# Key transposes in an attention decode kernel: one bf16 tile at a time in place of two packed as fp32

## The chip, the cores and the metric

The kernel runs on one core of one Trainium2 chip. Times are device microseconds of that core. A run that is over 1.5% above the fastest of its kernel counts as slow; ratios compare fast runs with fast runs, while medians are over all runs. TensorE's granted clock is given as a share of full speed; the traces show it at either 1.0 or 0.5, so a mean of 0.8 means that 40% of the time was spent at half speed (181.8 of 447.8 us in the profiled run of before; its clock record starts at 23.6 us, and what lies before counts as full speed).

## The reference, cut to what matters

Two attention layers, A and B, decode one token each for four sequences. Each has 32 query heads over 8 key heads. A attends to all 8192 cached keys, B to the last 2048. All tensors are bf16.

```python
q = (x @ wq).reshape(B, 1, 32, 128).transpose(0, 2, 1, 3)
scores = einsum("bhqd,bhkd->bhqk", q, k) * 128 ** -0.5
p = softmax(scores, axis=-1)
o = einsum("bhqk,bhkd->bhqd", p, v)
out = o.transpose(0, 2, 1, 3).reshape(B, 1, 4096) @ wo
```

The work on the key and value caches is split into 40 *units* of 2 MB of keys and 2 MB of values. Eight are B's; 32 are A's, one for each sequence and key head.

## The kernel before

The cached keys arrive with the key position on the partitions, but the score matmul needs the head dimension there, so TensorE transposes all keys. A unit has 64 key tiles of 128x128. The kernel takes them in eight groups of eight. It views two neighbouring bf16 tiles as one fp32 tile of 128x128 and transposes that, four times a group:

```python
def pe_T(u, k):                                   # unit u, group k
    ...
    for pi in range(4):
        t0 = k * 8 + 2 * pi
        ins = pe.transpose(out=bkf[:, pi * 128:(pi + 1) * 128],          # fp32 PSUM bank
                           in_=K_sbf[:, slot, t0:t0 + 2, :].rearrange("p t d -> p (t d)"),
                           identity=identf[:, :])
    ...
    # PSUM to SBUF: VectorE as int32 for even k, ScalarE as bf16 for odd k
```

A packed transpose puts pairs of head dimensions on one partition, so the query has to be rearranged to match. A small permutation matmul and split copies make `RQA` and `RQB`, and the scores of two tiles are the sum of two matmuls:

```python
for pi in range(4):
    for e in range(2):
        ins = pe.matmul(out=stb[:, t * CPT:(t + 2) * CPT], lhsT=ktv[:, pi, :, e],
                        rhs=rhs, start=(e == 0), stop=(e == 1))
```

The loads use four buffers each for K and V, in one queue.

## Time and profile before

| | before |
|---|---|
| time, median of the first three runs | 449.6 us (448.24 to 449.67) |
| span of the profiled run | 447.8 us |
| mean granted clock | 0.797 |
| TensorE instructions in one turn of the loop | 1316 |
| distance between packed transposes, clock 1.0 / 0.5 | 109 / 213 ns |

The last is the median distance between the starts of neighbouring matmuls of one group. Starts are the safer measure here, because the durations overlap: the mean duration of a packed transpose is 329 ns on the page below.

These are lines of the profile page: busy time of each engine; clock, DMA share and DMA rate in 40 slices of the span; the DMA queue that fetches instructions (packets, MB, share); and the four groups around the transpose (busy us, mean ns of one, then the idle time before them).

```profile
PE 373.4 (83%) x6783; PEld 339.4 (76%) x6783; DVE 195.9 (44%) x451; ACT 179.2 (40%) x202; POOL 40.1 (9%) x126
...
PEclk9996569989886899866596689867875986788596
DMA  8999999999999999999999999999999999999991
GB/s 337 411 415 438 413 421 415 420 421 423 423 422 421 425 422 425 424 429 427 427 427 430 430 424 426 430 428 427 429 426 427 426 430 429 426 424 430 430 403 65
...
q8 instruction: 22, 0.36, 0.3%
...
L341 ACT ACTIVATE KT_sb<-ps 128x1024 bf16<-128x1024 bf16 x160 | 163.0, 1023 | 244.9 <-PE ps L332 243.1
L332 PE MATMUL ps<-identf,K_sb 128*128 128x128 f32 x1280 | 217.1, 329 | 32.9 <-DMA K_sb<-in_A_k_cache_dram 17.5
L332 PEld LDWEIGHTS ps<-identf,K_sb 128*128 128x128 f32 x1280 | 179.0, 170 | 46.2 <-DMA K_sb<-in_A_k_cache_dram 18.6
L340 DVE COPY KT_sb<-ps 128x512 int32<-128x512 int32 x160 | 110.4, 690 | 138.9 <-PE ps L332 137.7
```

The next lines are of the table of windows: busy time of each engine in a stretch, then clock, DMA share and rate.

```profile
core 0: us, PE busy (x) PEld busy (x) DVE busy (x) ACT busy (x) POOL busy (x), PEclk, DMA share, GB/s
...
210.00:290.00 80.00, 72.22 (x1296) 67.13 (x1295) 35.61 (x82) 35.06 (x40) 7.50 (x24) 0.78 1.01 428
290.00:370.00 80.00, 73.63 (x1298) 67.85 (x1298) 35.52 (x82) 35.10 (x40) 7.17 (x24) 0.77 1.01 427
370.00:440.00 70.00, 63.30 (x1085) 57.25 (x1085) 32.03 (x73) 30.63 (x35) 6.74 (x21) 0.76 0.98 413
440.00:448.00 8.00, 5.17 (x126) 4.10 (x126) 2.08 (x7) 0.42 (x1) 0.46 (x2) 0.50 0.01 3
```

Read the DMA columns first. The DMA engines are nearly full from the first slice to the last but one, from the second on at 403 to 438 GB/s, and the kernel ends about 7 us after they go quiet. TensorE looks nearly full too, 72 of 80 us, but at a clock of 0.78 and with waits for keys among its idle time (17.5 us before the transposes). Such an engine may be a second limit or may have slack that was slowed down.

### The profile page before, as it was taken

The page shows a single profiled execution, that of the slowest core. Times are in us where ns is not written, and L with a number is a line of the kernel's source. Part 1 is how long each engine was busy: PE and PEld are TensorE (multiplying, and loading weights), DVE is VectorE, ACT ScalarE, POOL GpSimd, SP SyncE. Part 2 cuts the span into 40 slices and gives each one's busy share as a digit, 9 for nine tenths or more (in the row PEclk, how much of TensorE's full clock was granted, in tenths as well). Part 3 has the DMA queues.
Part 4 walks back from the last instruction along what each step waited for, and adds up shares of the span by engine and source line. Part 5 has one row for each costly group of instructions (what it writes and reads, how often), then busy time and mean ns, then how long its engine had stood idle before and what let it go on. Part 6 is the DMA issues. An engine that isn't in the chain of part 4 may idle for free.

```text
span 447.8 us, 14767 instructions
## 1 busy us (share of the span) xinstructions
PE 373.4 (83%) x6783; PEld 339.4 (76%) x6783; DVE 195.9 (44%) x451; ACT 179.2 (40%) x202; POOL 40.1 (9%) x126
## 2 busy tenths in 40 slices
PE   0685199899676999988998998899889998988997
PEld 0685199768561898878898887879878987878896
DVE  0354055656440455434363444344443544344363
ACT  1163045435330464434264434334442543435261
POOL 1100000001100011000010001000110100010010
PEclk9996569989886899866596689867875986788596
DMA  8999999999999999999999999999999999999991
GB/s 337 411 415 438 413 421 415 420 421 423 423 422 421 425 422 425 424 429 427 427 427 430 430 424 426 430 428 427 429 426 427 426 430 429 426 424 430 430 403 65
DMA packets 17270, 185.01 MB, mean 413 GB/s; under 512 B 1860, under 2 KB 2392, under 8 KB 4824
## 3 DMA queue, kind: packets, MB, share of 16 engines
q1 hardware_dynamic: 15096, 178.27, 94.4%
q10 hardware_dynamic: 2080, 6.30, 3.5%
q8 instruction: 22, 0.36, 0.3%
q14 instruction: 8, 0.07, 0.0%
q0 software_dynamic: 64, 0.01, 0.0%
HBM read 184.56 MB, written 0.01 MB: 412 GB/s over the span
## 4 chain that ended last, share of the span: by engine, by line
DMA 54%; PE 35%; issue 4%; ACT 3%; DVE 2%; POOL 0%; ACTq 0%; POOLq 0%
DMA K_sb<-in_A_k_cache_dram 41%; PE ps L332 19%; DMA W<-in_A_wq_dram 7%; DMA W<-in_B_wo_dram 6%; PE ps L397 6%; PE ps L371 5%; PE ps L483 3%; ACT KT_sb L341 3%; PE ps L278 1%; DVE KT_sb L340 1%; DVE Dt L543 0%; DVE M L505 0%; ACT PT L554 0%; PE ps L474 0%; PE ps L438 0%
## 5 line engine op out<-in xcount | busy, mean ns | idle before, releaser
L341 ACT ACTIVATE KT_sb<-ps 128x1024 bf16<-128x1024 bf16 x160 | 163.0, 1023 | 244.9 <-PE ps L332 243.1
L332 PE MATMUL ps<-identf,K_sb 128*128 128x128 f32 x1280 | 217.1, 329 | 32.9 <-DMA K_sb<-in_A_k_cache_dram 17.5
L332 PEld LDWEIGHTS ps<-identf,K_sb 128*128 128x128 f32 x1280 | 179.0, 170 | 46.2 <-DMA K_sb<-in_A_k_cache_dram 18.6
L340 DVE COPY KT_sb<-ps 128x512 int32<-128x512 int32 x160 | 110.4, 690 | 138.9 <-PE ps L332 137.7
L397 PE MATMUL ps<-PT,V_sb 128*128 128x4 bf16 (+1 forms) x2560 | 76.2, 165 | 3.6 <-DMA V_sb<-in_A_v_cache_dram 1.8
L371 PEld LDWEIGHTS ps<-RQc,KT_sb 128*128 128x128 bf16 x2048 | 72.9, 100 | 4.5 <-ACT KT_sb L341 1.2
L371 PE MATMUL ps<-RQc,KT_sb 128*128 128x8 bf16 x2048 | 74.3, 167 | 0.9 <-ACT KT_sb L341 0.8
L397 PEld LDWEIGHTS ps<-PT,V_sb 128*128 128x128 bf16 x2560 | 70.8, 97 | 3.9 <-DMA V_sb<-in_A_v_cache_dram 2.0
L575 POOL PARTITION_ALL_REDUCE LB<-L x40 | 17.3, 432 | 155.2 <-DVE L L566 155.2
L514 POOL PARTITION_ALL_REDUCE MB<-M x32 | 11.9, 371 | 173.3 <-DVE M L505 173.3
L483 PE MATMUL ps<-W,OL 128*4 128x512 bf16 x60 | 22.5, 537 | 4.8 <-DMA W<-in_B_wo_dram 4.8
L592 DVE TENSOR_TENSOR OTg<-ps,RL 128x4 bf16<-128x4 f32 (+1 forms) x40 | 6.9, 173 | 40.2 <-PE ps L397 40.2
L505 DVE TENSOR_REDUCE M<-ps 128x4 f32<-128x256 f32 (+1 forms) x40 | 19.1, 477 | 10.8 <-PE ps L371 10.8
L566 DVE TENSOR_REDUCE L<-PT 128x4 f32<-128x256 bf16 (+1 forms) x40 | 21.9, 547 | 3.3 <-ACT PT L554 2.8
L371 PE MATMUL ps<-RQB,KT_sb 128*128 128x16 bf16 x512 | 18.6, 171 | 2.1 <-issue 1.2
L371 PEld LDWEIGHTS ps<-RQB,KT_sb 128*128 128x128 bf16 x512 | 17.9, 99 | 3.0 <-issue 1.5
L554 ACT ACTIVATE PT<-Dt 128x256 bf16<-128x256 f32 (+1 forms) x40 | 18.1, 452 | 4.0 <-DVE Dt L543 2.0
L483 PEld LDWEIGHTS ps<-W,OL 128*4 128x4 bf16 x60 | 5.6, 104 | 15.3 <-issue 8.7
L278 PE MATMUL ps<-xT,W 128*128 128x4 bf16 x256 | 7.4, 165 | 10.9 <-DMA W<-in_A_wq_dram 10.6
L278 PEld LDWEIGHTS ps<-xT,W 128*128 128x128 bf16 x256 | 7.0, 101 | 11.1 <-DMA W<-in_A_wq_dram 10.7
L543 DVE TENSOR_TENSOR Dt<-ps,MB 128x256 f32<-128x256 f32 x32 | 13.3, 415 | 0.5 <-POOL MB L514 0.5
L257 PE MATMUL ps<-ident,xo_sb 4*128 4x4 bf16 x8 | 0.6, 170 | 14.2 <-POOL identf L617 14.2
(49 smaller groups left out, 64.6 us busy)
## 6 DMA issues: line engine op xcount, KB each, us to landing
K_sb<-in_A_k_cache_dram SPq DMA_DIRECT2D x32, 2048.0 KB, 32.0
V_sb<-in_A_v_cache_dram SPq DMA_DIRECT2D x31, 2048.0 KB, 36.0
K_sb<-in_B_k_cache_dram SPq DMA_DIRECT2D x16, 1024.0 KB, 28.2
V_sb<-in_B_v_cache_dram SPq DMA_DIRECT2D x16, 1024.0 KB, 28.2
W<-in_B_wq_dram SPq DMA_DIRECT2D x1, 4096.0 KB, 12.9
W<-in_A_wq_dram SPq DMA_DIRECT2D x1, 4096.0 KB, 30.0
W<-in_A_wo_dram ACTq DMA_DIRECT2D x8, 512.0 KB, 10.5
W<-in_B_wo_dram SPq DMA_DIRECT2D x1, 2048.0 KB, 29.1
```

The lines of the kernel that those rows point to most:

```text
L278: ins = pe.matmul(out=bk[:, hl * Bn:(hl + 1) * Bn], lhsT=W1wq[:, c, hq * DH:(hq + 1) * DH], rhs=xT[:, P, c, :], start=(c == 0), stop=(c == ...
L332: ins = pe.transpose(out=bkf[:, pi * 128:(pi + 1) * 128], in_=K_sbf[:, slot, t0:t0 + 2, :].rearrange("p t d -> p (t d)"), identity=identf[ ...
L340: return e.tensor_copy(out=KT_sb.bitcast(I32)[:, tj % NKT, :], in_=bkf.bitcast(I32)[:, :])
L341: return e.activation(out=KT_sb[:, tj % NKT, :], in_=bk[:, :], func=ACTF.Copy)
L371: ins = pe.matmul(out=stb[:, t * CPT:(t + 2) * CPT], lhsT=ktv[:, pi, :, e], rhs=rhs, start=(e == 0), stop=(e == 1))
L397: ins = pe.matmul(out=otb[:, s * CPT:(s + 1) * CPT], lhsT=V_sb[:, vs, t, :], rhs=pt_cols(u, t * CPT, CPT), start=(j == 0), stop=(j == J - 1))
L483: ins = pe.matmul(out=opb[0:Bn, 0:D], lhsT=OL[:, i // REP, i % REP, :], rhs=wo_view[:, wg + i // REP, i % REP, :], start=(P == 1 and first ...
L505: return dve.tensor_reduce(out=M1[:, 0:NC].rearrange("p (s h) -> p s h", h=CPT), in_=stb[:, 0:NT * CPT].rearrange("p (s j h) -> p s h j", ...
L543: return dve.tensor_tensor(out=Dt[:, 0:NT * CPT].rearrange("p (s j h) -> p s j h", s=S, h=CPT), in0=stb[:, 0:NT * CPT].rearrange("p (s j h ...
L554: return act.activation(out=PT[:, u % NPT, 0:NW], in_=Dt[:, 0:NW], func=ACTF.Exp, scale=scale)
L566: return dve.tensor_reduce(out=L1[:, 0:NC].rearrange("p (s h) -> p s h", h=CPT), in_=PT[:, u % NPT, 0:NT * CPT].rearrange("p (s j h) -> p ...
L575: return pool.partition_all_reduce(LB[:, 0:NC], L1[:, 0:NC], channels=128, reduce_op=ReduceOp.add)
```

## The change

The intent is to drop the packing: transpose the eight bf16 tiles one by one, use the query as it is, and remove the permutation matmul, its split copies and their set-up. Two things follow from it. The score matmuls keep their number but are half as wide (4 columns in place of 8 for A). And two matmuls of 512 columns that only add zeros to the projection's bank, and read `RQA` to do so, become eight of 128 columns. The core of the diff is here, with cuts marked:

```diff
-                for pi in range(4):
-                    t0 = k * 8 + 2 * pi
-                    ins = pe.transpose(out=bkf[:, pi * 128:(pi + 1) * 128],
-                                       in_=K_sbf[:, slot, t0:t0 + 2, :].rearrange("p t d -> p (t d)"),
-                                       identity=identf[:, :])
+                for i in range(8):
+                    ins = pe.transpose(out=bk[:, i * 128:(i + 1) * 128], in_=K_sb[:, slot, k * 8 + i, :], identity=ident[:, :])
 ...
-                for pi in range(4):
-                    t = k * 8 + 2 * pi
-                    for e in range(2):
-                        ...
-                        ins = pe.matmul(out=stb[:, t * CPT:(t + 2) * CPT], lhsT=ktv[:, pi, :, e],
-                                        rhs=rhs, start=(e == 0), stop=(e == 1))
+                for i in range(8):
+                    t = k * 8 + i
+                    ...
+                    ins = pe.matmul(out=stb[:, t * CPT:(t + 1) * CPT], lhsT=KT_sb[:, tj % NKT, i * 128:(i + 1) * 128],
+                                    rhs=rhs, start=True, stop=True)
 ...
-        def pe_job_perm(P):      # the permutation matmul and the copies into RQA and RQB; all of it goes
 ...
-            pool.memset(RQA[:, :, :, :, :], 0.0)
-            pool.memset(RQB[:, :, :, :, :, :], 0.0)
-            pool.memset(Dt[:, 0:128], 1.0)
```

More of the change, by code (lines that the diff above doesn't have):

```diff
@@ L112, in bass_concat_heads__gqa_block_cached__sliding_block_cached__decode_kernel @@
         onesb = sb("onesb", [128, 128], BF16)
-        identf = sb("identf", [128, 128], F32)
         NGQ = HQ // REP
         NGG = HKV // SB
-        RQA = sb("RQA", [128, Bn, NGQ, 2, 2 * REP], BF16)
-        RQB = sb("RQB", [128, Bn, NGG, 2, 2, 4 * REP], BF16)
-        RQc = sb("RQc", [128, Bn, 2, 2 * REP], BF16)
+        RQc = sb("RQc", [128, Bn, REP], BF16)
         zt = sb("zt", [128, Bn], BF16)
-        permE = sb("permE", [128, 2, 2, 64], BF16)
         MK = sb("MK", [128, 16], F32)
@@ L159, in bass_concat_heads__gqa_block_cached__sliding_block_cached__decode_kernel @@
         s_Eq, s_rq, s_opc = sm("s_Eq"), sm("s_rq"), sm("s_opc")
-        s_mk0, s_perm = sm("s_mk0"), sm("s_perm")
+        s_mk0 = sm("s_mk0")
         KTB = [0, 1, 2]
@@ L171, in bank_bf @@
             return banks_f[i].bitcast(BF16)
-        K_sbf = K_sb.bitcast(F32)
         W1wq = W1[:, :].rearrange("p (c n) -> p c n", c=DC)
@@ L203, in sem_of @@
             if t == "E":
-                if jobs[key[1]]["kind"] in ("xT", "QP", "perm"):
+                if jobs[key[1]]["kind"] in ("xT", "QP"):
                     return s_Eq
@@ L210, in sem_of @@
                 "ocp": s_ocp, "exp": s_exp, "ar1": s_ar1, "ar2": s_ar2, "setup": s_setup, "pset": s_setup,
-                "mk": s_mk, "acp": s_acp, "mk0": s_mk0, "perm": s_perm, "rq": s_rq, "OPJc": s_opc,
+                "mk": s_mk, "acp": s_acp, "mk0": s_mk0, "rq": s_rq, "OPJc": s_opc,
             }[t]
@@ L231, in bass_concat_heads__gqa_block_cached__sliding_block_cached__decode_kernel @@
         xt_idx = {}
-        perm_idx = {}
         ol_idx = {}
@@ L286, in pe_job_QP @@
             return dict(eng="dve", fn=efn, waits=[("T", idx)], inc=("E", idx))
-        def pe_job_perm(P):
-            idx = new_job("perm", "dve", P=P)
-            perm_idx[P] = idx
-            bk = bank_f(KTB[jobs[idx]["bank"]])
-            def fn(pe):
-                ins = None
-                for e in range(2):
-                    ins = pe.matmul(out=bk[:, e * Bn * HQ:(e + 1) * Bn * HQ],
-                                    lhsT=permE[:, e, :, :].rearrange("p t i -> p (t i)"),
-                                    rhs=QT[:, P, :, :].rearrange("p b h -> p (b h)"), start=True, stop=True)
-                return ins
-            op("pe", fn, waits=[("E", qp_idx[(P, NQP - 1)]), ("perm",), bankfree(idx)], inc=("T", idx))
-            def efn(dve):
-                ins = None
-                for e in range(2):
-                    for tl in range(2):
-                        src = bk[64 * tl:64 * tl + 64, e * Bn * HQ:(e + 1) * Bn * HQ]
-                        if P == 0:
-                            ins = dve.tensor_copy(
-                                out=RQA[64 * tl:64 * tl + 64, :, :, e, REP * tl:REP * tl + REP],
-                                in_=src.rearrange("p (b g h) -> p b g h", b=Bn, h=REP))
-                        else:
-                            ins = dve.tensor_copy(
-                                out=RQB[64 * tl:64 * tl + 64, :, :, :, e, 2 * REP * tl:2 * REP * tl + 2 * REP],
-                                in_=src.rearrange("p (b gg st c) -> p b gg st c", b=Bn, gg=NGG, c=2 * REP))
-                return ins
-            return dict(eng="dve", fn=efn, waits=[("T", idx)], inc=("E", idx))
         def pe_T(u, k):
@@ L324, in pe_T @@
             slot = u % NKS
-            bkf = bank_f(KTB[jobs[idx]["bank"]])
             def fn(pe):
                 ins = None
-                for pi in range(4):
-                    t0 = k * 8 + 2 * pi
-                    ins = pe.transpose(out=bkf[:, pi * 128:(pi + 1) * 128],
-                                       in_=K_sbf[:, slot, t0:t0 + 2, :].rearrange("p t d -> p (t d)"),
-                                       identity=identf[:, :])
+                for i in range(8):
+                    ins = pe.transpose(out=bk[:, i * 128:(i + 1) * 128], in_=K_sb[:, slot, k * 8 + i, :], identity=ident[:, :])
                 return ins
@@ L339, in efn @@
                 if eng == "dve":
-                    return e.tensor_copy(out=KT_sb.bitcast(I32)[:, tj % NKT, :], in_=bkf.bitcast(I32)[:, :])
+                    return e.tensor_copy(out=KT_sb.bitcast(I32)[:, tj % NKT, :], in_=bk.bitcast(I32)[:, :])
                 return e.activation(out=KT_sb[:, tj % NKT, :], in_=bk[:, :], func=ACTF.Copy)
@@ L347, in fn @@
             def fn(pool):
-                return pool.tensor_copy(out=RQc[:, u % Bn, :, :], in_=RQA[:, un["b"], un["hq0"] // REP, :, :])
-            return dict(eng="pool", fn=fn, waits=[("E", perm_idx[0])] + ([("S", (u - Bn) * NB + NB - 1)] if u - Bn >= NU_B else []),
+                return pool.tensor_copy(out=RQc[:, u % Bn, :], in_=QT[:, 0, un["b"], un["hq0"]:un["hq0"] + REP])
+            return dict(eng="pool", fn=fn, waits=[("E", qp_idx[(0, NQP - 1)])] + ([("S", (u - Bn) * NB + NB - 1)] if u - Bn >= NU_B else []),
                         inc=("rq", u))
@@ L357, in pe_S @@
             hqs = set()
-            ktv = KT_sb[:, tj % NKT, :].rearrange("p (i k e) -> p i k e", i=4, e=2)
             def fn(pe):
@@ L363, in fn @@
                 CPT = un["CPT"]
-                for pi in range(4):
-                    t = k * 8 + 2 * pi
-                    for e in range(2):
-                        if P == 0:
-                            rhs = RQc[:, u % Bn, e, :]
-                        else:
-                            rhs = RQB[:, b, un["gg"], t // J, e, :]
-                        ins = pe.matmul(out=stb[:, t * CPT:(t + 2) * CPT], lhsT=ktv[:, pi, :, e],
-                                        rhs=rhs, start=(e == 0), stop=(e == 1))
+                for i in range(8):
+                    t = k * 8 + i
+                    if P == 0:
+                        rhs = RQc[:, u % Bn, :]
+                    else:
+                        h0 = un["hq0"] + t // J * CPT
+                        rhs = QT[:, 1, b, h0:h0 + CPT]
+                    ins = pe.matmul(out=stb[:, t * CPT:(t + 1) * CPT], lhsT=KT_sb[:, tj % NKT, i * 128:(i + 1) * 128],
+                                    rhs=rhs, start=True, stop=True)
                 return ins
-            waits = [("E", tjob_idx[(u, k)]), ("rq", u) if P == 0 else ("E", perm_idx[P])]
+            waits = [("E", tjob_idx[(u, k)]), ("rq", u) if P == 0 else ("E", qp_idx[(P, NQP - 1)])]
             op("pe", fn, waits=waits, inc=("S", tj))
@@ L487, in pe_OPJ, with pe_zero, fn @@
             op("pe", fn, waits=waits, inc=("OPJ", gi))
-        def pe_open():
-            op("pe", lambda pe: pe.matmul(out=bank_f(OPB)[0:Bn, 0:D], lhsT=zt[:, :], rhs=RQA[:, :, :, :, :].rearrange("p b g e c -> p (b g e c)"),
-                                          start=True, stop=False),
-               waits=[("ocp", 1), ("E", perm_idx[0])])
-        def pe_close():
-            op("pe", lambda pe: pe.matmul(out=bank_f(OPB)[0:Bn, 0:D], lhsT=zt[:, :], rhs=RQA[:, :, :, :, :].rearrange("p b g e c -> p (b g e c)"),
-                                          start=False, stop=True), inc=("OPJc",))
+        def pe_zero(first):
+            def fn(pe):
+                ins = None
+                for c in range(D // 128):
+                    ins = pe.matmul(out=bank_f(OPB)[0:Bn, c * 128:(c + 1) * 128], lhsT=zt[:, :], rhs=onesb[:, :],
+                                    start=first and c == 0, stop=not first and c == D // 128 - 1)
+                return ins
+            op("pe", fn, waits=[("ocp", 1)] if first else [], inc=None if first else ("OPJc",))
         def dve_max(u):
@@ L614, in pool_setup1 @@
         def pool_setup1(pool):
-            ins = pool.affine_select(out=ident[:, :], in_=onesb[:, :], pattern=[[1, 128]],
-                                     compare_op=AluOpType.is_equal, fill=0.0, base=0, channel_multiplier=-1)
-            ins = pool.affine_select(out=identf[:, :], in_=Dt[:, 0:128], pattern=[[1, 128]],
-                                     compare_op=AluOpType.is_equal, fill=0.0, base=0, channel_multiplier=-1)
-            return ins
+            return pool.affine_select(out=ident[:, :], in_=onesb[:, :], pattern=[[1, 128]],
+                                      compare_op=AluOpType.is_equal, fill=0.0, base=0, channel_multiplier=-1)
         op("pool", pool_setup1, waits=[("pset",)], inc=("setup",))
@@ L628, in bass_concat_heads__gqa_block_cached__sliding_block_cached__decode_kernel @@
         op("dve", dve_setup0, inc=("mk0",))
-        def dve_setup1(dve):
-            ins = None
-            for e in range(2):
-                for tl in range(2):
-                    ins = dve.tensor_copy(out=permE[:, e, tl, :], in_=ident[:, :].rearrange("p (i e) -> p e i", e=2)[:, e, :])
-            return ins
-        op("dve", dve_setup1, waits=[("setup",)], inc=("perm",))
         for sh in range(2):
@@ L659, in bass_concat_heads__gqa_block_cached__sliding_block_cached__decode_kernel @@
             add(pe_job_QP(1, i))
-        add(pe_job_perm(1))
         def wo_load(eng, gi):
@@ L681, in bass_concat_heads__gqa_block_cached__sliding_block_cached__decode_kernel @@
         extra_jobs = {}
-        qa = [("xT", 0, 0)] + [("QP", 0, i) for i in range(NQP)] + [("perm", 0, 0)]
+        qa = [("xT", 0, 0)] + [("QP", 0, i) for i in range(NQP)]
         avail = list(range(1, NU_B)) or [0]
@@ L702, in bass_concat_heads__gqa_block_cached__sliding_block_cached__decode_kernel @@
             if u == LB0:
-                pe_open()
+                pe_zero(True)
             if u == LB1:
-                pe_close()
+                pe_zero(False)
             turn[0] = (u - LB0) // NLB if LB0 <= u < LB1 else None
@@ L745, in bass_concat_heads__gqa_block_cached__sliding_block_cached__decode_kernel @@
                             dve_after[anchor_after(i)].append(pe_job_xT(jb[1]))
-                        elif jb[0] == "perm":
-                            dve_after[anchor_after(i)].append(pe_job_perm(jb[1]))
                         else:
```

## The prediction

> **What bounds it now.** The DMA queues. On the profile page the 16 DMA engines are 9 tenths busy in nearly every slice at 420 to 430 GB/s; the table of windows shows a DMA share of 1.01 from 15 to 370 us, 0.98 from 370 to 440, 0.01 after. 185.01 MB at about 425 GB/s is 435 us; the rest is start-up and a tail of 7.6 us after the last V lands at about 440 us (118 PV matmuls, output projection, store).
>
> TensorE looks busy (PE 83%, PEld 76%) but has slack. From the starts of its first transposes, a unit (one batch and key head, 4 MB of K and V, 9.8 us of DMA) takes 7.15 to 7.5 us at full clock, 12.8 to 14.2 at half. Mean granted clock is 0.80: [...]part of "busy" is slack slowed down. The groups list has PE waiting 17.5 us for K of problem A. K loads take 31 us from issue to landing (view of the K tile), so about three units are queued and small PE delays do not starve DMA.
>
> **What changes on PE.** Start to start in the trace, a packed fp32 transpose takes 109 ns at full clock, 213 at half, for two key tiles. The only bf16 128x128 pairs (the permutation) are 55 ns apart at full clock. [...]
> - I expect 55: 64 x 55 = 3.52 us a unit for 32 x 109 = 3.49. [...]
> - Score matmuls keep their number (64 a unit, 25 ns apart): accumulating pairs become singles.
> - PSUM copies are the same: DVE 690 ns, ACT 1023 ns.
> - Gone: four permutation matmuls, eight DVE casts (2.3 us), permE copies (0.5), three memsets (1.2) and a select (0.28) on POOL. Off the critical path; perhaps 0.5 to 0.9 us before the first transpose at 19.0 us, which DMA runs through anyway.
> - PE has about 1,280 more matmuls and weight loads.
>
> **On the critical path:** nothing of size. Loads are unchanged in bytes, descriptors and order; the tail has no transposes after V lands. It may move by tenths through instruction fetch (a gap of 0.82 us under "issue" stands at 439.4).
>
> **Time:** 449.3 us; 446.8 to 452.5 in 8 of 10. Faster by over 2%: 0.01; within 2%: 0.94; slower by over 2%: 0.05.
>
> **What would show it.** DMA share 1.01 at 420 to 430 GB/s through 370 us; last V at 440; 2560 transposes, 55 ns apart at full clock and 107 at half, eight lasting as long as four packed ones; ACT's copies 163 and DVE's 110 us unchanged; permutation and RQA/RQB lines gone.
>
> **What would make it wrong.** The clock. Streams of matmuls 4 to 16 columns wide seem not to raise it (the last 118 PV matmuls ran back to back at half clock), so the transposes must keep it up. [...] If bf16 ones did not count, units would take 13 to 14 us and PE would bound at over 500 us. Second: a bf16 stream at over 90 ns, bringing PE level with DMA.

The forecast of 449.3 us rests on 435 us of loads with start-up and tail, and on 3.52 us of transposes a unit in place of 3.49, an estimate from the distances of 55 and 109 ns in the trace. That the clock drops after waits for data was the author's reading; the trace also has drops without them (under a_light and b_light).

## More of the kernel before

TensorE's program for units 10 to 37 is a hardware loop of seven turns with four units in each; only TensorE's program is looped:

```python
with nc.Fori(0, len(turns), engines=[mybir.EngineType.PE]):
    run(turns[0])
    ...
```

## The result, and the profile after

| | before | after |
|---|---|---|
| time, median of 4 runs | 449.63 us (448.24 to 449.84) | 450.01 us (449.85 to 450.92) |
| span of the profiled run | 447.8 us | 449.2 us |
| mean granted clock, profiled run | 0.797 | 0.765 |
| TensorE matmuls | 6783 | 8065 |
| TensorE instructions in one turn | 1316 | 1572 |
| distance between transposes, clock 1.0 / 0.5 | 109 / 213 ns | 56 / 107 ns |

The ratio of after to before is 1.0019, with a 95% interval of 0.9995 to 1.0044: the same time. A ratio here is the mean time of one kernel's fast runs over that of the other's of the same rounds, so it is not quite the ratio of the medians.

The same lines of the page, of the kernel after:

```profile
PE 377.1 (84%) x8065; PEld 348.6 (78%) x8065; DVE 193.9 (43%) x439; ACT 178.8 (40%) x202; POOL 38.5 (9%) x122
...
PEclk9996555569695976689589569658768986788597
DMA  8999999999999999999999999999999999999991
...
q8 instruction: 26, 0.43, 0.4%
...
L300 ACT ACTIVATE KT_sb<-ps 128x1024 bf16<-128x1024 bf16 x160 | 163.0, 1025 | 250.8 <-PE ps L293 249.0
L293 PE MATMUL ps<-ident,K_sb 128*128 128x128 bf16 x2560 | 220.6, 258 | 30.2 <-DMA K_sb<-in_A_k_cache_dram 12.5
L293 PEld LDWEIGHTS ps<-ident,K_sb 128*128 128x128 bf16 x2560 | 194.1, 118 | 41.1 <-DMA K_sb<-in_A_k_cache_dram 13.3
L299 DVE COPY KT_sb<-ps 128x512 int32<-128x512 int32 x160 | 110.4, 690 | 137.0 <-PE ps L293 136.3
```

And its table of windows, with the same columns:

```profile
210.00:290.00 80.00, 73.90 (x1631) 68.92 (x1628) 36.82 (x85) 36.02 (x41) 7.44 (x24) 0.76 1.01 428
290.00:370.00 80.00, 72.33 (x1554) 68.10 (x1554) 35.61 (x83) 35.01 (x40) 7.44 (x24) 0.77 1.01 427
370.00:440.00 70.00, 63.38 (x1300) 58.52 (x1301) 31.52 (x73) 30.71 (x35) 6.38 (x20) 0.76 0.98 415
```

DMA share and rate are the same to the last digit in the two long windows. TensorE has twice as many transposes in about the same busy time (220.6 us in place of 217.1). The copies out of PSUM have not moved.

How long two neighbouring groups take at full clock is seen in the timeline. The first line is of before (eight packed transposes), the second of after (sixteen):

```profile
427.98 1.07 PE L332 MATMUL ps<-identf,K_sb 128*128 128x128 f32 x8
```

```profile
437.55 1.05 PE L293 MATMUL ps<-ident,K_sb 128*128 128x128 bf16 x16
```

So the change is neutral in TensorE work, and the DMA bound would hide a small difference anyway. The first transpose starts at 18.3 us, 0.7 us earlier than before (19.0), because the permutation is gone. The loads run through that stretch, so nothing is gained by it.

The profiled run of the kernel after is the slowest of its four, and its span is 1.4 us longer than that of before. That shift is there when the last value matmuls begin, at 441.60 us in place of 440.17 (the line of before is shown under a_half); the last values landed at 442.3 us in place of 440.6. It is within the scatter: the four runs lie 1.6 us apart before and 1.1 us after.

```profile
441.60 3.29 PE L354 MATMUL ps<-PT,V_sb 128*128 128x4 bf16 x120 [1.21 <-issue]
```

### The profile page after: what moved, and what is told of

Same layout as the page of the kernel before. It is cut to its first block, busy times and chain, and to the rows that moved or that the text cites. A ratio compares the mean times of both kernels' runs of the same rounds, so it can differ in the third digit from the quotient of the medians.

```text
span 449.2 us, 17315 instructions
## 1 busy us (share of the span) xinstructions
PE 377.1 (84%) x8065; PEld 348.6 (78%) x8065; DVE 193.9 (43%) x439; ACT 178.8 (40%) x202; POOL 38.5 (9%) x122
## 4 chain that ended last, share of the span: by engine, by line
DMA 50%; PE 44%; ACT 2%; issue 1%; DVE 1%; SPq 0%; ACTq 0%
DMA K_sb<-in_A_k_cache_dram 34%; PE ps L293 26%; PE ps L354 7%; DMA W<-in_A_wq_dram 7%; PE ps L328 6%; DMA W<-in_B_wo_dram 6%; DMA K_sb<-in_B_k_cache_dram 4%; PE ps L440 3%; ACT KT_sb L300 2%; PE ps L272 1%; PE ps L431 0%; PE ps L395 0%; DVE KT_sb L299 0%; SPq L592 0%; PE ps L450 0%
## 5 line engine op out<-in xcount | busy, mean ns | idle before, releaser
L300 ACT ACTIVATE KT_sb<-ps 128x1024 bf16<-128x1024 bf16 x160 | 163.0, 1025 | 250.8 <-PE ps L293 249.0
L293 PE MATMUL ps<-ident,K_sb 128*128 128x128 bf16 x2560 | 220.6, 258 | 30.2 <-DMA K_sb<-in_A_k_cache_dram 12.5
L293 PEld LDWEIGHTS ps<-ident,K_sb 128*128 128x128 bf16 x2560 | 194.1, 118 | 41.1 <-DMA K_sb<-in_A_k_cache_dram 13.3
L299 DVE COPY KT_sb<-ps 128x512 int32<-128x512 int32 x160 | 110.4, 690 | 137.0 <-PE ps L293 136.3
L328 PE MATMUL ps<-RQc,KT_sb 128*128 128x4 bf16 x2048 | 74.8, 165 | 2.8 <-issue 2.0
L328 PEld LDWEIGHTS ps<-RQc,KT_sb 128*128 128x128 bf16 x2048 | 68.8, 99 | 4.5 <-issue 2.1
L328 PE MATMUL ps<-QT,KT_sb 128*128 128x8 bf16 x512 | 19.0, 168 | 4.0 <-issue 2.8
L328 PEld LDWEIGHTS ps<-QT,KT_sb 128*128 128x128 bf16 x512 | 17.8, 102 | 4.5 <-issue 2.9
L403 DVE CAST OL<-ps 32x16 bf16<-32x16 f32 (+1 forms) x36 | 6.5, 181 | 13.2 <-PE ps L395 12.8
```

Of the source, the lines that this page charges most:

```text
L293: ins = pe.transpose(out=bk[:, i * 128:(i + 1) * 128], in_=K_sb[:, slot, k * 8 + i, :], identity=ident[:, :])
L299: return e.tensor_copy(out=KT_sb.bitcast(I32)[:, tj % NKT, :], in_=bk.bitcast(I32)[:, :])
L300: return e.activation(out=KT_sb[:, tj % NKT, :], in_=bk[:, :], func=ACTF.Copy)
L328: ins = pe.matmul(out=stb[:, t * CPT:(t + 1) * CPT], lhsT=KT_sb[:, tj % NKT, i * 128:(i + 1) * 128], rhs=rhs, start=True, stop=True)
```

## The experiments

The theory has three parts.

1. The DMA queues bound the kernel, and TensorE has slack.
2. A packed fp32 transpose costs TensorE just what two bf16 ones cost.
3. The transposes keep TensorE's clock up, in bf16 as in fp32.

The rivals are that TensorE, 83% busy, is a limit as well, so that the equal time is a balance of a gain and a loss there; and that the two forms differ on TensorE, with the DMA bound hiding it. All kernels below but `a_half` and the four "light" ones compute the right result. `a_` variants start from the kernel after, `b_` variants from the kernel before. Turns are measured between the loop's branches in the trace.

### Less transpose work: a_half

```diff
-                for i in range(8):
+                for i in (range(8) if u == 0 else range(4)):
```

> The kernel after, with only four of the eight bf16 transposes of each group from the second unit on (the rest of the bank is stale, so the result is wrong on purpose). A warm unit on TensorE should fall from 7.1 us to about 5.4 us. Theory (the DMA queues bound the kernel, TensorE has slack): the time stays within 1% of the kernel after, 446 to 450.5 us; at most about 3 us are saved in the tail, where TensorE works through the last two units after their keys have landed. Rival (TensorE, 84% busy on the page, is the limit or half of it): transposes are 58% of its busy time, so halving them saves 40 us or more, to about 400 to 410 us.

Measured: 447.66 us (447.42 to 447.81), ratio to before 0.996 (0.9935 to 0.9984). The output check let this kernel pass although half of its transposed keys are stale, so a passed output check says little about the keys here. One window, a turn of the loop:

```profile
260.20:300.60 40.40, 31.64 (x650) 28.16 (x649) 17.75 (x41) 17.36 (x20) 3.71 (x12) 0.54 1.01 427
```

A turn still takes 40.4 us at 427 GB/s. Half of the transposes are worth 0.4%, not 40 us, so the rival that TensorE is the limit falls. What TensorE gained, it lost in clock: 0.54 in place of about 0.78.

The 0.4% comes from the end. These are timeline lines of TensorE from 440 us in the kernel before, whose last values landed at 440.6 us:

```profile
440.17 3.31 PE L397 MATMUL ps<-PT,V_sb 128*128 128x4 bf16 x118 [0.82 <-issue]
443.79 1.86 PE L474 MATMUL ps<-W,OTg 128*4 128x256 bf16 x8 [0.31 <-DVE OTg L592]
```

The same stretch of a_half:

```profile
440.46 0.38 PE L354 MATMUL ps<-PT,V_sb 128*128 128x4 bf16 x9 [0.24 <-issue]
441.11 0.59 PE L354 MATMUL ps<-PT,V_sb 128*128 128x4 bf16 x16 [0.27 <-DMA V_sb<-in_A_v_cache_dram]
442.00 1.87 PE L431 MATMUL ps<-W,OTg 128*4 128x256 bf16 x8 [0.31 <-DVE OTg L549]
```

In a_half the value matmuls keep pace with the landing values, and only 16 are left for the last quarter. In the kernel before TensorE is behind, and 118 of them stand after 440 us. The last units' transposes are thus on the path that ends last, but together with everything else they are worth only about 2 us.

### More transpose work: a_x15, a_x2, b_x2

```diff
-                for i in range(8):
+                for i in [0, 1, 2, 3, 0, 1, 2, 3, 4, 5, 6, 7]:      # a_x15; a_x2: [*range(8), *range(8)]
```

b_x2 does the same to the four packed transposes: `for pi in [*range(4), *range(4)]`.

> The kernel after, with twelve transposes a group in place of eight (four are done twice; the result stays right). Adds 32 x 55 ns = 1.76 us of TensorE work a unit, to about 8.9 us warm, still under the 9.8 us that the DMA queues need for a unit's keys and values. Theory (slack): 447 to 453 us, and the mean granted clock rises from about 0.77 to 0.85 or more[...]. Rival (TensorE is the limit): 40 x 1.76 = 70 us more, about 520 us.

> The kernel after, with every transpose done twice (result right). Adds 64 x 55 ns = 3.5 us a unit, to about 10.7 us warm, over the 9.8 us of DMA. Theory (slack of about 2.7 us a unit): the slack is used up and TensorE binds: 465 to 495 us, mean clock 0.95 or more, DMA share below 1. Rival (TensorE is the limit now): 450 + 140 = 590 us.

> The kernel before, with every packed fp32 transpose done twice (result right). Adds 32 x 109 ns = 3.5 us a unit. Theory (a packed transpose costs just what two bf16 ones cost): within 1% of the run that doubles the bf16 transposes. Rival (the packing is cheaper or dearer on TensorE and the DMA bound hides it): differs from that run by several per cent[...].

| run | time, median of all runs | ratio of fast runs | TensorE instructions a turn | packets of the instruction queue in each turn |
|---|---|---|---|---|
| a_x15 | 560.05 us | 1.2497 (1.2418 to 1.2577) | 1828 | 9 |
| a_x2 | 591.3 us | 1.3049 (1.2932 to 1.3165) | 2084 | 10 |
| b_x2 | 508.16 us | 1.1325 (1.1292 to 1.1357) | 1572 | 0 |

Two expectations failed: a_x15 should have cost nothing, and a_x2 should have taken 465 to 495 us and equalled b_x2. (Two of the four runs of a_x15 and of a_x2 count as slow, a_x2's profiled run among them; its trace is used only for its counts.) Taken alone, a_x15 speaks for the rival. Its profile does not. These are lines of its page:

```profile
q8 instruction: 85, 1.39, 1.0%
...
PE 69%; issue 15%; DMA 14%; ACT 1%; DVE 1%; SPq 0%
...
L293 PE MATMUL ps<-ident,K_sb 128*128 128x128 bf16 x3840 | 277.5, 238 | 61.8 <-issue 52.3
```

And this is TensorE's timeline after a jump back to the start of the loop, which stands at 258.1 us:

```profile
264.21 3.38 PE L293 MATMUL ps<-ident,K_sb 128*128 128x128 bf16 x30 [6.93 <-issue]
269.46 2.08 PE L293 MATMUL ps<-ident,K_sb 128*128 128x128 bf16 x18 [1.86 <-issue]
```

For comparison, b_x2 after a jump back at 292.4 us:

```profile
292.64 3.60 PE L332 MATMUL ps<-identf,K_sb 128*128 128x128 f32 x31 [0.96 <-issue]
```

TensorE waits under "issue", for nothing that the profile shows: 6.93 and 1.86 us after this jump, against 0.96 us in b_x2. The instruction queue has moved 85 packets of 16 KB in place of 26, and in each turn 9 of them fall. In the kernels before and after, none and one fall between the first jump back and the last. So in a_x15 instructions are fetched anew in every turn; that they are TensorE's is inferred, since only TensorE's program is looped and longer. What sets the length of the wait, no run here tests; the DMA engines were 0.80 busy over a whole turn (313.5 to 366.6 us). The repeated transposes had made the loop body longer, and two causes were mixed: work and code size. The next two runs separate them.

### Work without code, code without work: b_x15 and a_tiny

```diff
 # b_x15: as much extra work as a_x15, in a shorter loop
-                for pi in range(4):
+                for pi in [0, 1, 0, 1, 2, 3]:
 # a_tiny: the code size of a_x15, with little work
+                for i in range(4):
+                    ins = pe.transpose(out=bk[:, i * 128:i * 128 + 4], in_=K_sb[0:4, slot, k * 8 + i, :], identity=ident[0:4, 0:4])
```

> The kernel before, with six packed fp32 transposes a group in place of four (two are done twice; result right). It adds 32/2 x 109 ns = 1.74 us of TensorE work a unit, as much as the run with twelve bf16 transposes a group did, but the loop body has only 1444 TensorE instructions a turn (that run: 1828, before: 1316, after: 1572). Theory (slack, and the 1.25 times of that run came from fetching the loop's instructions anew in every turn): 447 to 453 us, 22 to 30 instruction DMAs on queue 8, clock up from 0.78 to 0.85 or more. Rival (TensorE has no slack for 1.74 us a unit): 500 us or more.

> The kernel after, with four transposes of 4x128 added to each group: they write again what the full ones write, so the result is right. They bring the loop body to 1828 TensorE instructions a turn, but only 32 x 25 ns = 0.8 us of work a unit. Theory[...]: as slow as the run with twelve full transposes, 530 to 565 us, some 85 instruction DMAs on queue 8, idle time of TensorE under issue. Rival (that run was slow from its added work): 0.8 us a unit lies within the slack, 448 to 453 us.

(What is tested is whether the length of the loop, not the work, costs the time.)

Measured: b_x15 takes 452.11 us, ratio 1.0041 (1.0019 to 1.0063); a_tiny takes 614.24 us, ratio 1.3677 (1.3602 to 1.3752). First the instruction queue and one turn of b_x15, then those of a_tiny:

```profile
q8 instruction: 24, 0.39, 0.4%
...
230.20:268.20 38.00, 36.11 (x713) 34.76 (x713) 18.05 (x41) 17.61 (x20) 3.77 (x12) 1.00 1.01 428
```

```profile
q8 instruction: 84, 1.38, 0.9%
...
274.60:336.20 61.60, 52.92 (x906) 46.47 (x905) 17.75 (x41) 17.59 (x20) 3.71 (x12) 0.50 0.72 282
```

b_x15 carries half as many transposes again, 7.0 us more work a turn at full clock (64 x 109 ns), and loses 0.4%. The clock pays for it: 1.00 in that turn, against 0.78 in the same stretch of the kernel before. This is the slack. a_tiny adds little work (128 narrow transposes a turn, an estimated 3.2 us at the 25 ns between score matmuls of 4 columns at full clock) and is the slowest of all. Its time lies above the expected 530 to 565 us, because its clock also fell, to 0.50 in the turn shown (TensorE is busy for 52.9 us of it, against 39.5 us of a turn of 53.1 us at clock 0.90 in a_x15). So a_x15 was slow from its code size, not its work.

The turns that ran at a clock of 1.00 without fetching give TensorE's own cost of an unchanged turn:

| run | turn at clock 1.00 | added transposes a turn | left |
|---|---|---|---|
| b_x15 | 38.0 us | 64 x 109 ns = 7.0 us | 31.0 us |
| b_x2 | 44.95 us | 128 x 109 ns = 14.0 us | 31.0 us |
| a_x11 (below) | 36.3 us | 96 x 56 ns = 5.4 us | 30.9 us |

The turns of b_x2 and a_x11, by the table of windows:

```profile
292.40:337.30 44.90, 43.10 (x777) 41.76 (x777) 17.74 (x41) 17.60 (x20) 3.76 (x12) 1.00 0.94 386
```

```profile
239.30:275.60 36.30, 34.28 (x873) 33.14 (x873) 18.04 (x41) 17.61 (x20) 3.73 (x12) 1.00 1.01 428
```

At full clock both forms need about 31 us a turn, and the loads need 40.4 us (a_half). TensorE has about 9.4 us of slack a turn; 7.0 us more fit, and 14.0 do not (45 us a turn).

### How much room is left in the loop: a_x10 and a_x11

```diff
-                for i in range(8):
+                for i in [0, 1, 0, 1, 2, 3, 4, 5, 6, 7]:      # a_x10; a_x11: [0, 1, 2, 0, 1, 2, 3, 4, 5, 6, 7]
```

> The kernel after with ten transposes a group (two done twice, result right): 1700 TensorE instructions in a turn of the loop, against 1572 that were not fetched again and 1828 that were. If the loop body still fits: 448 to 453 us, no instruction DMAs on queue 8 within the turns, 26 to 28 in all. If not: some 8 of them a turn and over 520 us; then the change left less than 128 instructions of room. [...]

> The same with eleven transposes a group: 1764 TensorE instructions a turn. Fits: 448 to 455 us. Does not fit: over 530 us with 8 or 9 instruction DMAs a turn. With the run of ten it brackets the edge to 64 or 128 instructions.

One run each, of unknown state. "Fits" in these expectations means no more than that a turn is not fetched anew. a_x10 (1700 instructions a turn) took 531.84 us, with 9 packets of the instruction queue in each of the six turns measured. a_x11 (1764) took 481.26 us; two of its six turns had 9 packets and lasted 53.3 and 48.3 us, and the other four had none and lasted 36.3 to 38.6 us. So a_x11 met neither of its two expected times, and the longer loop fetched less often. The edge is not a plain number of instructions: it lies somewhere between 1572, which was never fetched anew, and 1700, which always was, and above it the outcome varies. Why, these runs do not show.

### Taking the DMA bound away: a_light and b_light

```diff
+            part = 0 if u >= NU_B + NKS else None
-            op("sp", dma(kv_dst(K_sb, u % NKS, u), kv_src(KC[units[u]["P"]], u)), waits=waits, inc=("K", u))
+            op("sp", dma(kv_dst(K_sb, u % NKS, u, part), kv_src(KC[0], u, part)), waits=waits, inc=("K", u))
 # and the same for V
```

> The kernel after, with K and V loads of problem A cut to a quarter from its fifth unit on (the rest of each slot is stale, the result is wrong on purpose). The DMA queues should go idle and TensorE bind. Expected: 370 to 400 us, a turn of four units in 29 to 31 us in place of 40 us, clock near 1.0. Theory (both forms cost TensorE the same): within 1% of the same cut of the kernel before. Rival (a difference that the DMA bound hid): over 2% apart.

> The kernel before with the same cut of the K and V loads (result wrong on purpose). Expected: 370 to 400 us, a turn of four units in 29 to 31 us, clock near 1.0, transposes 109 ns apart. Theory: within 1% of the same cut of the kernel after. Rival: over 2% apart.

One turn of a_light and about one of b_light:

```profile
252.60:286.70 34.10, 32.25 (x777) 30.74 (x777) 17.75 (x41) 17.48 (x20) 3.73 (x12) 0.90 0.41 138
```

```profile
251.30:285.00 33.70, 32.70 (x650) 30.07 (x649) 17.75 (x41) 17.52 (x20) 3.77 (x12) 0.91 0.41 141
```

The DMA share is 0.41, so TensorE binds, and a_light is 7% faster than before (ratio 0.9271, 0.9243 to 0.9299): the loads did bound the kernel. Medians are 416.28 us (a_light, 415.17 to 418.26) and 416.29 us (b_light, 411.86 to 420.4). b_light falls apart into two runs near 412 us at a clock of 0.856 and two near 420 us at 0.818, and only the first two count as fast. Against their mean of 412.4 us, a_light's mean of 416.5 us is 1.0% more; against all four there is no difference. A difference of over 2%, as the rival wanted, is not there; one of about 1% is neither shown nor excluded.

The expected 370 to 400 us and a clock near 1.0 were wrong. In these loops TensorE never waits for keys or values, only for copies out of PSUM and under "issue" (3.6 and 3.9 us in four turns of a_light, 218 to 355 us), yet the clock still drops once or twice a turn (mean 0.90 in the turn shown), and a turn takes about 34 us, not 29 to 31. So the clock also falls without waits for loads. The kernel before says the same: of the 16 drops between 180 and 441 us, nine had a wait for keys or values in the 7 us before them, three had idle time under "issue", and four had no idle time of 0.05 us or more there. What makes it fall stays open.

### What sets the pace of a transpose: b_light_n64 and a_light_n64

```diff
+                    nk = 128 if u == 0 else 64
-                    ins = pe.transpose(out=bkf[:, pi * 128:(pi + 1) * 128],
-                                       in_=K_sbf[:, slot, t0:t0 + 2, :].rearrange("p t d -> p (t d)"),
-                                       identity=identf[:, :])
+                    ins = pe.transpose(out=bkf[:, pi * 128:pi * 128 + nk],
+                                       in_=K_sbf[0:nk, slot, t0:t0 + 2, :].rearrange("p t d -> p (t d)"),
+                                       identity=identf[0:nk, 0:nk])
```

> The lightened kernel before, each packed fp32 transpose from the second unit on over 64 keys only (identity 64x64: half the moving width, but weights of 128 columns as before; result wrong on purpose). If the 109 ns between packed transposes are the weight load, they stay 109 ns apart at full clock; if they are the moving stream, 55.

> The lightened kernel after with the same cut (64 keys, identity 64x64). If the 55 ns between bf16 transposes are the moving stream, they come to 27 to 30 ns; if they are the weight load, they stay 55.

One run each (416.25 and 410.75 us, state unknown). The clock was at 0.5 throughout the loop, so spacings are compared there: packed fp32 107 ns in place of 213, bf16 53 ns in place of 107. (About 90 bf16 distances and 40 fp32 ones fell at full clock. Their medians are 29 ns, against 56, and 63 ns, against 109: the fp32 one is more than half, and why is open.) Both follow the moving width, not the 128 columns of weights. So the moving stream appears to set the pace, and an fp32 column takes twice the time of a bf16 one (213 against 107 ns for 128 columns). That would be why two tiles packed as fp32 gain nothing over two single ones. One reservation: the cut also halves the rows of the weights, and no run here tests whether those count.

The clock is the surprise. A turn of b_light_n64, then one of a_light_n64:

```profile
251.80:286.60 34.80, 33.91 (x650) 30.03 (x649) 17.76 (x41) 17.59 (x20) 3.75 (x12) 0.50 0.41 135
```

```profile
252.00:285.50 33.50, 32.60 (x778) 29.22 (x777) 17.77 (x41) 17.60 (x20) 3.73 (x12) 0.50 0.43 141
```

TensorE is hardly ever idle (33.9 of 34.8 us), yet it is held at half clock, and with half of the transpose work a turn takes about as long as with all of it (34.1 us at 0.90). Transposes 64 columns wide and matmuls 4 or 8 columns wide, back to back, did not raise the clock (0.50); with transposes 128 wide in place of 64 it rose (0.90 and 0.91 in the turns above). bf16 ones do this as well as fp32 ones: a_light ran at 0.83 to 0.84, b_light at 0.82 to 0.86. In a_half, with half as many transposes of full width, the clock fell to 0.54 too. So these runs do not tell whether the width counts or the number of columns in all.

None of the twelve runs beats both kernels with a right result. a_half is 0.4% faster and the four light runs 7 to 9%, but all five leave work out.

## Why the prediction was right, and where it was thin

- **"The DMA queues" bound it.** Right. Halving the transposes left a turn at 40.4 us and 427 GB/s (a_half), and half as many again cost 0.4% (b_x15).
- **TensorE "has slack"; part of "busy" is slack slowed down.** Right: about 31 us of work a turn at full clock against 40.4 us of loads. The 7.15 to 7.5 us read for a unit give 28.6 to 30 us a turn; the measured 31 also holds the projection, the small jobs and about 1 us of "issue" at the loop's jump.
- **"I expect 55".** Right to 1 ns: 56 ns at full clock and 107 at half. The prediction did not say why the forms are equal; the n64 runs point to the moving stream.
- **The score matmuls, the PSUM copies and the removed work.** Right: ACT 163.0 and DVE 110.4 us are unchanged, there are 1282 more matmuls (1280 transposes and six of the zero-adding ones more, four permutation ones fewer), and the first transpose starts 0.7 us earlier without effect on the time.
- **"Nothing of size" on the critical path.** Right in size. Transposes do lie on it in the last two units, where TensorE works behind the loads; a_half puts what they can give at about 2 us.
- **"The clock" as the main danger.** The danger did not arrive: bf16 transposes ran 56 ns apart with the clock at 1.0. The clock did move with the transposes: 0.54 in a turn with half of them (a_half), about 0.78 with all, 1.00 with half as many again (b_x15) or three more a group (a_x11), and 0.50 with transposes 64 columns wide. What it follows is not shown. The 118 matmuls that ran at half clock are 4 columns wide; for 8 columns there are only the n64 runs, and for 16 nothing.
- **Instruction fetch, "by tenths".** By size this held: the idle time under "issue" before the last value matmuls went from 0.82 to 1.21 us. That a fetch causes it is not shown: the nearest packets of the instruction queue ran from 437.6 to 438.7 and from 441.2 us before (the wait: 439.35 to 440.17), from 439.2 to 440.3 and from 442.7 us after (440.4 to 441.6). No turn of the loop fetched its instructions anew. But the prediction counted 1,280 more matmuls without asking what they do to the loop. They lengthen its body from 1316 to 1572 instructions; at 1700 the kernel with ten transposes a group took 532 us. That the change stayed on the safe side was luck as far as the prediction goes: the dangers that it named were the clock and a slow bf16 stream, not code size.

## What to carry to other kernels

Before costing an edit on a busy engine, find its cost at full clock by adding work until the time moves; here 83% busy hid about 9.4 us of slack in 40.4. A change that trades few wide instructions for many narrow ones may be neutral in work and still cost code size in a loop (here 1572 instructions a turn in place of 1316; the kernel with 1700 took 532 us): count the instructions of a turn, and look at the instruction queue's packets and at idle time under "issue". An experiment that repeats instructions changes both work and code, so add a run that changes only one of them.
